# A gated mix of a long convolution and an MLP on one core: all 1,099 steps in a new order, with new evacuation engines and ring slots

## The chip, the core and the metric

The kernel runs on one core of a Trainium2 chip. A core has TensorE (PE) for matmuls, VectorE (DVE), ScalarE (ACT), GpSimd (POOL) and the queue of SyncE (SP), which here issues nearly all DMA transfers. Each engine works through its own list of instructions in order; semaphores make an instruction wait for what it reads or overwrites. The metric is the device time of one execution in microseconds (us). Lower is better. Names such as L707 are lines of the kernel's file.

## The reference, cut to what matters

```python
def _A_ref(q, k, v, shift_k, ssm_k, ssm_D):          # B, S, D = 1, 2048, 640
    for t in range(4):                                # causal 4-tap shift convolution of k
        k_shift = k_shift + k_pad[:, t:t + S, :] * shift_k[:, 3 - t][None, None, :]
    kv = k_shift * v
    ...
    y = irfft(rfft(kv, 2 * S) * rfft(ssm_k, 2 * S))[:S]   # long causal convolution, per channel
    y = y + kv * ssm_D[None, None, :]
    return q * y

def _B_ref(x, w1, w2, w3, w4):                        # w1, w2: 640x640; w3: 640x1536; w4: 1536x640
    h = _gelu(_layernorm(x) @ w1)
    hs = (the four quarters of h, shifted by 1, -1, 2, -2 in time) @ w2
    x1 = x + hs
    return x1 + _gelu(_layernorm(x1) @ w3) @ w4

x = A_q
g = _sigmoid((x * gate_w).sum(-1, keepdims=True))
return g * _A_ref(x, A_k, A_v, A_shift_k, A_ssm_k, A_ssm_D) + (1 - g) * _B_ref(x, B_w1, B_w2, B_w3, B_w4)
```

All tensors are bf16; the output is 1 x 2048 x 640. (B_x isn't used.)

## The kernel before

**Tiling.** Time (2048) is 128 partitions times 16 rows t1 (`NT`). The 16 rows come in four blocks c of four rows, a block being one 640 KB transfer. Channels are 5 groups of 128. A program of named steps does the work; a name such as `x_norm.2.AAVV:1` is the builder `x_norm`, its arguments (block 2, engines AAVV) and the number k of the step within it.

**Start-up, both branches.** `load_x0`, `load_x`, `k_load.c:0` and `v_load` bring in x, k and v. `x_stats` makes the layernorm's sums of a block, row by row: on DVE for a letter V, on ACT for a letter A as a square and a copy, each with a sum (L666 to L698); its last step raises to a power on POOL. `x_norm` writes the normalised rows, on ACT or DVE by letter. `x_turn` transposes a block into `xt`: for blocks 0 and 1 with PE and evacuations of up to eight 128 x 128 pieces (`transposed`, L610), for blocks 2 and 3 with the letter D as one DMA transposition on SP (L652). `k_load.c:1` to `:6` transpose a block of k in the same way, and `tap` forms the four-tap convolution of 128 channels with 76 small row-tiled matmuls (L590); each quarter of its result is multiplied by v either by DVE from PSUM (letter V, `both`, L605) or by an ACT copy (`copied`, L599) and a DVE product (`times`, L602). `mlp1.c.u` is one product of block c with 128 columns of w1 in PSUM, five matmuls (L707), and a gelu on ACT (L710).

**The long convolution** is a Fourier transform in two stages of matmuls. `step1.KV` and `step1.HT0` (filter: `load_h`, `h_transpose`) apply table F1 and send the results to scratch in DRAM, `S_x` and `S_h` (L437). `gather.x.s` and `gather.h.s` read them back transposed, 640 KB each, into a ring of four buffers "ax" (L440 to L446). `step2` applies table CMP, `product` multiplies the spectra, `step3` goes back by table INV and sends to `S_g`, `gin` reads that, `step4` applies F4 and multiplies by the gate and by q (`load_q`). The tables are made on the chip: `f1_table`, `t2_table`, `i_tables`, `f4_table` end in a sine on ACT (L277). Sine and gelu need different tables of ACT's own, which it loads when the function changes (ACT_TABLE_LOAD).

**The MLP.** `h_shift` on POOL shifts the quarters of h; `w2.t1` makes x1 in two halves, adds x on DVE (L791) and takes the squares' sum on ACT (L797). `x1_norm` ends with a DMA transposition into `x1t` (L821). `w3.c.f` is a product like mlp1, with gelu into `gt` (L840, L844); `w4.t1` sums 12 matmuls for each half row (L867) and adds to X1 on DVE (L870). `scale_x1`, `gate` and `store` finish.

**Order.** Python runs the steps in the order of the tuple `ORDER` (from L911, `emit` at L2022), inside `tc.manual_schedule` (L2034), so each engine's queue has its instructions in that order and nothing reorders them. A step that issues on several engines issues on all of them at its place. SP's transfers, stores and transpositions are one queue too.

**Ring slots.** `slot()` takes the next character of `SLOTS[tag]` each time a buffer with that tag is asked for: "c" are the eight PSUM banks, "row" four row buffers (k blocks, normalised rows, staging, gates), "gt" four gelu buffers, "xt" two, "gq" three, "ax" four gather buffers, "hp" four spectra. A buffer can be written once all readers of the tile that had this slot before are done; that wait is put on the instruction that writes first.

**Evacuation.** The letters A and V in a step's name choose ACT or DVE for each copy out of PSUM (`evac`, L358).

Of the kernel before, what the change touches and what calls it, by code (L numbers as in the profile page):

```python
# [41 lines left out]
def kernel(  # L42
# [836 lines left out]
    def step4(t1, ev):  # L879
# [32 lines left out]
        "open.L1.left:0 "  # L912
        "open.A2.right:0 "
        "consts0:0 "
        "load_x0.0:0 "
        "warm:0 "
        "load_x0.1:0 "
        "consts0:1 "
        "warm:1 "
        "warm:2 "  # L920
        "pow0:0 "
        "kv_alloc:0 "
        "k_load.3.AVA:0 "
        "f4_table:0 "
        "x_stats.0.VVVA:0 "
        "warm:3 "
        "k_load.3.AVA:1 "
        "x_stats.0.VVVA:1 "
        "load_x.1:0 "
        "x_stats.0.VVVA:2 "  # L930
        "k_load.3.AVA:5 "
        "x_stats.0.VVVA:3 "
        "x_stats.0.VVVA:4 "
        "x_stats.0.VVVA:5 "
        "x_stats.0.VVVA:6 "
        "warm:4 "
        "row_order:0 "
        "k_load.2.VAV:0 "
        "f1_table:0 "
        "x_norm.0.VVAA:0 "  # L940
        "x_norm.0.VVAA:1 "
        "f4_table:1 "
        "x_stats.1.VVVV:0 "
        "k_load.3.AVA:2 "
        "load_x.3:0 "
        "x_norm.0.VVAA:2 "
        "x_stats.1.VVVV:1 "
        "k_load.3.AVA:3 "
        "x_turn.0.AAA:0 "
        "k_load.3.AVA:6 "  # L950
        "k_load.2.VAV:5 "
# [1113 lines left out]
```

## Time and profile before

| | us |
|---|---|
| median of 3 runs | 227.58 (227.55 to 228.22) |
| the profiled execution | 227.13 |
| its span, first to last instruction | 225.4 |
| PE busy in the span | 217.8 |
| DVE busy | 183.7 |
| ACT busy | 171.4 |
| POOL busy | 38.1 |
| moved by DMA | 57.61 MB |

The granted TensorE clock is 1.000 over the span. In the views, "busy" is the time in which an engine executes; a group's row gives the line, engine, operation, output and input with shapes, the count, then busy time and mean of one in ns, then the idle time of the engine just before these instructions and what ended most of it. A row of the timeline gives start, duration, engine and line. In square brackets stand the idle time before an instruction and what released it. PEld is the loading of weights into PE, which overlaps its matmuls; SPq and ACTq are the queues' own times.

### The profile page before, as it was taken

The numbers are of one execution on the slowest core, as the hardware profiler recorded it, in microseconds if no ns is written. First come the engines' busy times: TensorE is split into PE (matmuls) and PEld (weight loads), VectorE is DVE, ScalarE is ACT, GpSimd is POOL, SyncE is SP. The second block draws the span as 40 slices with busy tenths as digits, with TensorE's granted clock in tenths as the row PEclk, the third lists the DMA queues.
The fourth block names the chain that finished last, engine by engine and source line by source line (L and its number), as shares of the span: only waits on it lengthen the run. The fifth ranks groups of instructions, "written<-read, shape, count | busy, mean of one in ns | idle before, by whom it ended". The sixth has DMA issues, their size and how long they took to land.

```text
span 225.4 us, 6053 instructions
## 1 busy us (share of the span) xinstructions
PE 217.8 (97%) x2427; PEld 121.5 (54%) x2428; DVE 183.7 (81%) x447; ACT 171.4 (76%) x341; POOL 38.1 (17%) x91
## 2 busy tenths in 40 slices
PE   8989999899999999999999999999999999999994
PEld 2557455447846563345664444556533547657762
DVE  7898998868889969963899988989999841439994
ACT  4899988787999999999987597967988450266450
POOL 4247246816000431300600000000000000000000
PEclk9999999999999999999999999999999999999999
DMA  6999998892998999999989570690794879429914
GB/s 226 374 376 344 258 280 170 317 364 107 361 365 355 348 295 265 410 334 343 254 219 338 116 243 0 191 379 17 119 305 166 249 259 366 175 60 305 324 70 179
DMA packets 41770, 57.61 MB, mean 256 GB/s; under 512 B 18446, under 2 KB 34446, under 8 KB 41486
## 3 DMA queue, kind: packets, MB, share of 16 engines
q1 hardware_dynamic: 41166, 54.60, 75.4%
q0 software_dynamic: 576, 2.62, 3.1%
q8 instruction: 19, 0.31, 0.6%
q14 instruction: 9, 0.07, 0.1%
HBM read 34.93 MB, written 18.35 MB: 236 GB/s over the span
## 4 chain that ended last, share of the span: by engine, by line
PE 79%; DMA 9%; DVE 4%; ACT 4%; issue 1%; POOL 1%; SPq 0%; ACTq 0%
PE ps L840 24%; PE ps L867 23%; PE psw L788 7%; PE ps L465 5%; PE ps L893 4%; DMA X<-in_A_q_dram 4%; PE psm L707 4%; DMA xt<-xn 3%; PE psz L228 3%; PE ps L512 3%; PE ps L423 2%; PE pst L390 2%; DVE X L791 2%; ACT stg L360 2%; DMA S_x<-stg 2%; PE psk L590 1%
## 5 line engine op out<-in xcount | busy, mean ns | idle before, releaser
L840 PE MATMUL ps<-x1t,W 128*128 128x512 bf16 x240 | 56.1, 380 | 0.1
L867 PE MATMUL ps<-W,gt 128*128 128x320 bf16 (+2 forms) x383 | 55.1, 299 | 0.1
L867 PEld LDWEIGHTS <-gt 128*128 128x128 bf16 x384 | 36.2, 98 | 17.7 <-issue 3.0
L844 ACT ACTIVATE gt<-ps 128x512 bf16<-128x512 f32 x48 | 27.6, 609 | 19.0 <-PE ps L867 10.6
L840 PEld LDWEIGHTS <-W 128*128 128x128 bf16 x240 | 21.9, 98 | 28.7 <-issue 5.9
L360 ACT CAST stg<-ps 128x512 bf16<-128x512 f32 x55 | 28.6, 604 | 2.3 <-PE ps L423 2.0
L870 DVE SCALAR_TENSOR_TENSOR X<-ps,OMG,X 128x320 bf16<-128x320 f32 (+2 forms) x32 | 17.2, 547 | 11.9 <-PE ps L867 11.7
L707 PE MATMUL psm<-xt,WA 128*128 128x512 bf16 x100 | 23.4, 379 | 1.9 <-DMA WA<-in_B_w_dram 0.8
L360 ACT CAST gs<-ps 128x320 bf16<-128x320 f32 x41 | 15.6, 440 | 8.8 <-PE ps L512 4.8
L788 PE MATMUL psw<-WA,HT 128*128 128x320 bf16 x116 | 21.4, 300 | 0.0
L362 DVE CAST XS<-ps 128x512 bf16<-128x512 f32 x19 | 12.5, 684 | 6.7 <-PE ps L465 6.7
L362 DVE CAST stg<-ps 128x512 bf16<-128x512 f32 x25 | 15.8, 683 | 1.9 <-PE ps L423 1.9
L707 PEld LDWEIGHTS <-WA 128*128 128x128 bf16 x100 | 9.2, 97 | 12.9 <-DMA WA<-in_B_w_dram 1.0
L360 ACT CAST hs<-ps 128x512 bf16<-128x512 f32 x28 | 15.0, 605 | 1.4 <-PE ps L465 1.4
L791 DVE SCALAR_TENSOR_TENSOR X<-psw,X 128x320 bf16<-128x320 f32 x32 | 14.5, 487 | 1.6 <-PE psw L788 1.6
L897 ACT ACTIVATE y<-ps,GS 128x320 bf16<-128x320 f32 x22 | 10.4, 526 | 5.7 <-PE ps L893 3.5
L710 ACT ACTIVATE HT<-psm 128x512 bf16<-128x512 f32 x20 | 11.8, 617 | 3.6 <-PE psm L707 3.5
L788 PEld LDWEIGHTS <-HT 128*128 128x128 bf16 x116 | 10.7, 98 | 6.8 <-issue 3.1
L362 DVE CAST gs<-ps 128x320 bf16<-128x320 f32 x23 | 10.7, 484 | 2.4 <-PE ps L512 1.7
L797 ACT ACTIVATE jk<-X 128x640 bf16<-128x640 bf16 x16 | 12.2, 761 | 0.5 <-DVE X L791 0.4
L788 PE MATMUL psw<-WA,HM 128*128 128x320 bf16 x44 | 12.3, 299 | 0.0
L360 ACT CAST XS<-ps 128x512 bf16<-128x512 f32 x21 | 11.8, 607 | 0.5 <-PE ps L465 0.3
(151 smaller groups left out, 346.6 us busy)
## 6 DMA issues: line engine op xcount, KB each, us to landing
S_x<-stg SPq DMA_DIRECT2D x8, 640.0 KB, 4.3
S_h<-stg SPq DMA_DIRECT2D x8, 640.0 KB, 4.8
ax<-S_x SPq DMA_DIRECT2D x8, 640.0 KB, 5.9
ax<-S_h SPq DMA_DIRECT2D x8, 640.0 KB, 8.1
S_g<-gs SPq DMA_DIRECT2D x8, 640.0 KB, 3.6
W<-in_B_w_dram SPq DMA_DIRECT2D x2, 1920.0 KB, 9.1
kn<-in_A_k_dram SPq DMA_DIRECT2D x4, 640.0 KB, 6.9
E<-in_A_ssm_k_dram SPq DMA_DIRECT2D x5, 512.0 KB, 6.1
```

The source lines that it names most:

```text
L360: A.copy(out=dst, in_=src)
L362: V.tensor_copy(out=dst, in_=src)
L465: PE.matmul(ps[j][q:q + 32, lo - 512 * u:hi - 512 * u], lhsT=CMP[HALF[j], 8 * b + 4 * h + i, c, :], rhs=st[name, 2 * b + h][HALF[j], i, lo ...
L707: PE.matmul(ps[:].rearrange("p (a b) -> p a b", a=4), lhsT=W1N[:, k, 160 * u:160 * u + P] if u < 4 else W1M[:, k, :], rhs=xt[:, :, k, :], ...
L710: A.activation(out=st["HT"][:, 4 * c:4 * c + 4, u, :], in_=ps[:].rearrange("p (t b) -> p t b", t=4), func=ACT.Gelu_apprx_tanh)
L788: PE.matmul(ps[:], lhsT=h_tile(f, t1), rhs=W2P[:, f, o:o + W], start=(f == 0), stop=(f == 4))
L791: V.scalar_tensor_tensor(out=X1[:, t1, o:o + W], in0=box["ps"][:], scalar=1.0, in1=X[:, t1, o:o + W], op0=ALU.mult, op1=ALU.add, accum_out ...
L797: A.activation(out=jk[:], in_=X1[:, t1, :], func=ACT.Square, accum_out=S12[:, 1, t1:t1 + 1])
L840: PE.matmul(ps[:].rearrange("p (a b) -> p a b", a=4), lhsT=st["W3"][:, k, f * P:(f + 1) * P], rhs=xt[:, :, k, :], start=(k == 0), stop=(k ...
L844: A.activation(out=st["gt", c, f // 4][:, f % 4, :], in_=ps[:], func=ACT.Gelu_apprx_tanh)
L867: PE.matmul(ps[:], lhsT=st["gt", c, f // 4][:, f % 4, i * P:(i + 1) * P], rhs=st["W4"][:, f, o:o + w], start=(f == 0), stop=(f == FC - 1))
L870: V.scalar_tensor_tensor(out=X1[:, t1, o:o + w], in0=box["ps"][:], scalar=OMG[:, t1:t1 + 1], in1=X1[:, t1, o:o + w], op0=ALU.mult, op1=ALU ...
```

## The change

Two places of the file change: `SLOTS` and `ORDER`. Every step of before is in the new order once, and none is added, but for the letters: how many evacuations of a kind ACT does goes, before to after, from 12 to 5 in `tap`, 22 to 17 in `step4`, 41 to 38 in `step3`, 21 to 19 in `step2.x`, 28 to 29 in `step2.h`, 27 to 25 in `step1.KV`, 28 to 29 in `step1.HT0`, 3 to 6 in `x_norm`, 6 to 8 in `x1_norm`, 3 to 5 in `x_turn`, 6 to 5 in `k_load` and 2 to 3 in `h_transpose`. The ring "gq" is asked for 22 times instead of 34, since each letter A of `tap` and `step4` needs a buffer. The slots are dealt anew: each new buffer takes the one that has been free longest at its place in the order. The number of buffers stays.

```diff
     SLOTS = {
-        "c": "012345670124703510347205142356401723605162370514731057423671045261304732641374153670421350627413"
...
+        "c": "012345670254602167053253210657432170413547021630627501432675140326573410267451306427103542673542"
...
-        "row": "01230213021302320123012031203120310310303",
-        "gt": "012301031010231012301201",
+        "gt": "012302201231230102312301",
+        "row": "01230213201320312031023122103120321021020",
         "xt": "010101",
-        "gq": "0120201201021020120122102121021021",
-        "ax": "0123120312030213",
-        "hp": "01231302",
+        "gq": "0122010200120201021012",
+        "ax": "0123031203123120",
+        "hp": "01230312",
     }
```

Of the order, the new one in its core (the old one is printed one step to a line from L911):

```diff
+        "open.L1.left:0 open.A2.right:0 kv_alloc:0 warm:0 load_x0.1:0 warm:1 consts0:0 consts0:1 warm:2 warm:3 "
+        "warm:4 load_x0.0:0 f4_table:0 load_x.3:0 k_load.0.AAA:0 k_load.0.AAA:3 x_stats.0.VVVA:0 x_stats.0.VVVA:1 "
+        "x_stats.0.VVVA:2 x_stats.0.VVVA:3 load_x.1:0 f4_table:1 x_stats.0.VVVA:4 k_load.0.AAA:1 x_stats.0.VVVA:5 "
+        "k_load.0.AAA:5 x_stats.0.VVVA:6 k_load.3.VVV:0 x_stats.3.VVAA:0 x_stats.3.VVAA:1 x_stats.3.VVAA:2 "
+        "x_stats.3.VVAA:3 x_stats.3.VVAA:4 x_stats.3.VVAA:5 x_norm.0.AVAV:0 x_norm.0.AVAV:1 x_turn.0.AAA:0 "
+        "x_norm.0.AVAV:2 x_norm.0.AVAV:3 x_turn.0.AAA:4 k_load.0.AAA:2 k_load.1.AVA:0 row_order:0 x_turn.0.AAA:5 "
+        "x_stats.1.VVVV:0 x_stats.1.VVVV:1 x_stats.3.VVAA:6 k_load.3.VVV:3 k_load.3.VVV:1 x_stats.3.VVAA:7 "
+        "x_turn.0.AAA:2 x_turn.0.AAA:1 k_load.3.VVV:4 k_load.1.AVA:5 x_turn.0.AAA:3 x_stats.1.VVVV:2 k_load.1.AVA:6 "
...
+        "k_load.0.AAA:4 k_load.1.AVA:4 k_load.3.VVV:2 load_w1.0:0 mlp1.0.0:0 mlp1.0.0:1 k_load.3.VVV:6 "
+        "x_norm.1.VVAV:0 mlp1.0.1:0 v_load.0:0 x_norm.1.VVAV:1 x_norm.1.VVAV:2 x_norm.1.VVAV:3 k_load.0.AAA:6 "
+        "load_w1.1:0 mlp1.0.3:0 w1_mixed:0 k_load.2.VVV:0 k_load.2.VVV:5 k_load.2.VVV:3 k_load.2.VVV:1 "
+        "x_turn.1.VAA:4 z_cols:0 x_turn.1.VAA:2 mlp1.0.1:1 x_turn.1.VAA:5 x_turn.1.VAA:3 x_norm.3.VVVA:0 mlp1.0.3:1 "
+        "x_norm.3.VVVA:1 x_turn.1.VAA:0 x_norm.3.VVVA:2 x_norm.3.VVVA:3 mlp1.0.4:0 x_turn.1.VAA:1 v_load.1:0 "
+        "mlp1.0.4:1 mlp1.1.0:0 k_load.1.AVA:2 k_wrap:0 mlp1.1.2:0 mlp1.1.0:1 mlp1.1.1:0 load_cj:0 mlp1.1.2:1 "
+        "k_load.2.VVV:2 mlp1.1.1:1 k_load.2.VVV:6 k_load.2.VVV:4 kv_consts:0 tap.3.AVVA:0 tap.3.AVVA:7 tap.4.AVVV:0 "
+        "tap.3.AVVA:1 tap.4.AVVV:5 tap.4.AVVV:3 tap.4.AVVV:1 load_x.2:0 x_turn.3.D:0 mlp1.1.4:0 x_stats.2.VVAA:0 "
+        "tap.3.AVVA:3 mlp1.3.0:0 x_stats.2.VVAA:1 x_stats.2.VVAA:2 x_stats.2.VVAA:3 x_stats.2.VVAA:4 v_load.2:0 "
...
+        "x_stats.2.VVAA:7 load_w2:0 load_h.2:0 load_h.1:0 tap.3.AVVA:4 mlp1.3.0:1 d_fold:0 mlp1.3.3:0 mlp1.3.3:1 "
+        "mlp1.3.4:0 mlp1.3.4:1 h_shift.3:0 tap.3.AVVA:2 tap.0.AVVV:0 x_norm.2.AAVV:0 x_norm.2.AAVV:1 "
+        "x_norm.2.AAVV:2 h_shift.0:0 tap.0.AVVV:5 tap.0.AVVV:7 tap.0.AVVV:8 tap.1.VVAV:0 tap.1.VVAV:1 tap.1.VVAV:3 "
+        "tap.1.VVAV:7 mlp1.0.2:0 tap.1.VVAV:5 tap.0.AVVV:1 x_norm.2.AAVV:3 mlp1.3.1:0 tap.1.VVAV:2 tap.0.AVVV:6 "
+        "mlp1.0.2:1 f1_table:1 tap.1.VVAV:4 h_shift.3:1 tap.2.VVVV:0 tap.2.VVVV:1 tap.2.VVVV:7 tap.0.AVVV:3 "
+        "tap.0.AVVV:4 mlp1.3.1:1 mlp1.1.3:0 mlp1.1.3:1 tap.0.AVVV:2 tap.1.VVAV:8 tap.1.VVAV:6 "
+        "step1.KV.3.AAVAAAVVAV:6 step1.KV.3.AAVAAAVVAV:7 tap.2.VVVV:3 x_turn.2.D:0 tap.2.VVVV:2 mlp1.2.3:0 "
+        "step1.KV.3.AAVAAAVVAV:8 mlp1.2.3:1 mlp1.2.0:0 tap.2.VVVV:4 load_h.4:0 mlp1.2.0:1 tap.2.VVVV:5 tap.2.VVVV:6 "
...
+        "gather.x.0:0 step2.x.0.AVVVAAVVAV:13 w2.14:0 w2.9:1 w2.14:1 i_tables:6 w2.11:0 w2.11:1 w2.13:2 "
+        "step2.x.3.AVVVVVAAVV:7 w2.4:2 swap.L1.L2.left:0 w2.4:3 w3.0.11:0 w3.0.1:0 w2.8:4 w3.0.4:0 w3.0.3:0 w2.6:4 "
+        "w3.0.11:1 w3.0.1:1 w2.13:3 gate:0 w3.0.4:1 step2.x.3.AVVVVVAAVV:1 step2.x.3.AVVVVVAAVV:12 "
...
+        "step2.x.3.AVVVVVAAVV:14 w2.10:4 w2.11:4 w2.9:4 x1_norm.2.VAAA:0 x1_norm.2.VAAA:1 step2.x.0.AVVVAAVVAV:7 "
+        "step2.x.0.AVVVAAVVAV:1 step2.x.0.AVVVAAVVAV:11 step2.x.0.AVVVAAVVAV:10 step2.x.0.AVVVAAVVAV:3 "
+        "step2.x.0.AVVVAAVVAV:5 w3.0.10:0 w3.0.7:0 w3.0.10:1 w3.0.7:1 w3.0.9:1 w3.0.6:0 load_w4:0 x1_norm.2.VAAA:2 "
+        "w3.0.5:0 w3.0.6:1 step2.x.3.AVVVVVAAVV:3 scale_x1.3.V:0 step2.x.3.AVVVVVAAVV:4 gather.h.7:0 "
+        "step2.h.3.AVAAVAAVAV:12 step2.h.3.AVAAVAAVAV:14 step2.x.3.AVVVVVAAVV:5 step2.x.3.AVVVVVAAVV:9 w3.0.5:1 "
+        "w4.2:0 step2.x.3.AVVVVVAAVV:10 step2.h.3.AVAAVAAVAV:13 step2.x.0.AVVVAAVVAV:4 x1_norm.1.VVAV:2 "
+        "x1_norm.1.VVAV:3 step2.x.3.AVVVVVAAVV:11 gather.h.6:0 step2.h.3.AVAAVAAVAV:3 step2.h.3.AVAAVAAVAV:9 "
...
+        "step2.h.3.AVAAVAAVAV:1 w4.1:1 gather.h.0:0 step2.h.3.AVAAVAAVAV:2 step2.h.0.AAAAAAAAAA:0 "
+        "step2.h.0.AAAAAAAAAA:1 step2.h.0.AAAAAAAAAA:2 product.7:1 product.7:2 scale_x1.8.V:0 product.7:3 "
+        "gather.h.1:0 product.7:4 step2.h.0.AAAAAAAAAA:12 w4.0:2 w4.0:3 step2.h.0.AAAAAAAAAA:14 "
...
+        "step2.h.2.AVAVAVAVAA:6 step2.h.2.AVAVAVAVAA:7 step2.h.2.AVAVAVAVAA:8 w4.5:2 w4.5:3 step2.h.2.AVAVAVAVAA:11 "
+        "w4.6:0 w4.6:1 x1_norm.3.VAAA:6 w4.7:0 step3.2.VVVVAAAA:5 step3.2.VVVVAAAA:8 step2.h.2.AVAVAVAVAA:10 "
+        "w3.2.5:0 w3.2.8:0 w3.2.6:0 product.5:0 w3.2.5:1 step3.2.VVVVAAAA:7 step3.2.VVVVAAAA:6 pow0:0 "
...
+        "w4.13:3 step4.12.AA:6 store.6:0 w4.15:0 w4.15:1 w4.15:3 store.7:0 w4.14:0 w4.14:1 w4.14:2 w4.14:3 "
+        "store.8:0 store.8:1 close.L2:0 close.C:0"
```

SP's first transfers, before: `load_x0.0`, `load_x0.1`, `k_load.3`, `load_x.1`, `k_load.2`, `load_x.3`, `load_w1.1`, `load_w1.0`, `k_load.0`, `k_load.1`, `load_x.2`, `load_cj`, `d_fold`, `x_turn.3.D`. After: `load_x0.1`, `load_x0.0`, `load_x.3`, `k_load.0`, `load_x.1`, `k_load.3`, `k_load.1`, `load_w1.0`, `load_w1.1`, `k_load.2`, `load_cj`, `load_x.2`, `x_turn.3.D`, `load_gw`, `load_w2`, `load_h.2`, `load_h.1`, `d_fold`, `x_turn.2.D`. PE's nine products of mlp1 ahead of `tap.3` become seven, and `pow0`, which stood among the first steps, is now one of the later ones.

More of the change, by code (lines that the diff above doesn't have):

```diff
@@ L911 @@
     ORDER = (
[L912 to L951, printed above, removed]
@@ L2008 @@
-        "store.8:1 "
-        "close.L2:0 "
-        "close.C:0 "
[170 rows of a table added]
     ).split()
```

1064 lines of the change are left out of this document (4 added, 1060 removed), and 127 rows, old and new, of the table ORDER.

## The prediction, made before the changed kernel ran

> **What bounds the kernel now.** I read the page's busy shares first, then the stretches of the span, then what TensorE (PE) waits for, then the chain that ended last and the first 42 us line by line.
>
> ```profile
> PE 217.8 (97%) x2427; PEld 121.5 (54%) x2428; DVE 183.7 (81%) x447; ACT 171.4 (76%) x341; POOL 38.1 (17%) x91
> PE 79%; DMA 9%; DVE 4%; ACT 4%; issue 1%; POOL 1%; SPq 0%; ACTq 0%
> ```
>
> PE is busy 97% of the span, and 79% of the last chain is PE. The change keeps every matmul, so what it can win is PE's idle time and little else. The stretches (start:end, length, busy time of PE, PEld, DVE, ACT, POOL, granted clock, DMA share, GB/s) say where that is.
>
> ```profile
> 0.98:8.30 7.32, 7.32 (x21) 2.59 (x21) 6.59 (x35) 4.57 (x8) 2.92 (x9) 1.00 0.85 304
> 8.30:14.20 5.90, 4.39 (x64) 3.69 (x63) 5.28 (x19) 5.24 (x7) 0.51 (x4) 1.00 1.06 378
> 14.20:27.70 13.50, 13.48 (x105) 7.77 (x105) 12.66 (x38) 13.44 (x27) 7.43 (x10) 1.00 1.02 325
> 27.70:41.50 13.80, 12.39 (x412) 7.80 (x412) 12.83 (x37) 12.10 (x25) 8.71 (x23) 1.00 0.92 223
> 41.50:85.00 43.50, 43.40 (x357) 25.96 (x358) 35.86 (x104) 38.79 (x76) 11.73 (x21) 1.00 0.89 318
> 85.00:130.00 45.00, 44.85 (x515) 21.93 (x512) 37.33 (x76) 39.22 (x81) 6.52 (x21) 1.00 0.94 282
> 130.00:221.40 91.40, 91.34 (x964) 51.32 (x955) 72.00 (x141) 57.79 (x123) 0.00 (x0) 1.00 0.62 202
> ```
>
> Idle is 1.51 us in 8.3 to 14.2 (5.90 less 4.39), 1.41 in 27.7 to 41.5, and 0.10, 0.15 and 0.06 in the three long stretches, 0.31 together. So about 3.2 us could be won. In the first two stretches the DMA engines are full (share 1.06 and 0.92), and ACT is busy 13.44 of 13.50 us between them: the start-up hangs on transfers and on ACT, the other 180 us on PE alone.
>
> ```profile
> PE psm L707 <- DMA WA<-in_B_w_dram: 0.8, 1, 0.8
> PE psm L707 <- ACT yk L599: 0.8, 1, 0.8
> PE pst L619 <- DMA kn<-in_A_k_dram: 0.7, 1, 0.7
> PE psm L707 <- DMA xt<-xn: 0.2, 1, 0.2
> ```
>
> Transfers cost PE 0.8, 0.7 and 0.2, thus 1.7 us: all that a plan with longer transfers can save here.
>
> **The start-up, step by step.** Before, x0, k.3, x.1, k.2, x.3 and the w1 halves are loaded in that order; after, x0, x.3, k.0, x.1, k.3, k.1, w1. The arrivals are read off the first instruction that waited for each:
>
> ```profile
> 4.36 0.74 ACT L679 ACTIVATE jk<-X 128x640 bf16<-128x640 bf16 x1 [2.36 <-DMA X<-in_A_q_dram]
> 5.22 0.74 ACT L681 ACTIVATE jk<-X 128x640 bf16<-128x640 bf16 x1
> 8.29 0.86 PE L619 MATMUL pst<-IDB,kn 128*128 128x128 bf16 x12
> 9.85 0.89 DVE L685 BATCH_NORM_STATS2 b<-X 128x6 f32<-128x320 bf16 x2 [0.32 <-DMA X<-in_A_q_dram]
> 11.42 0.68 PEld L619 LDWEIGHTS <-kn 128*128 128x128 bf16 x12 [0.89 <-DMA kn<-in_A_k_dram]
> 14.22 3.41 PE L707 MATMUL psm<-xt,WA 128*128 128x512 bf16 x15 [0.82 <-DMA WA<-in_B_w_dram]
> ```
>
> The third transfer is there at 8.3, the fourth at 9.85, the fifth at 11.4. In the changed kernel the third is x.3, and its four statistics passes on ACT (x_stats.3, two blocks of a square and a sum) stand ahead of x_norm.0. A pass takes 0.86 from start to start (4.36 to 5.22), so ACT is free at 8.3 + 4 × 0.86 = 11.7. Behind them wait, on ACT, two of x_norm.0's rows and the copies that free x.0's transposes for mlp1:
>
> ```profile
> 9.97 0.82 ACT xn L662
> 10.79 0.47 ACT KT L360
> 12.09 0.91 ACT xt L360
> 24.32 7.63 DMA xt<-xn
> 32.00 3.41 PE psm L707 x15
> 41.46 2.33 PE psm L707 x10
> ```
>
> Two rows 1.64, two half copies and three whole ones, 2 × 0.47 + 3 × 0.91 = 3.2: 16.6 for the first product against 14.22 before. By then PE has done one more block of K transposes:
>
> ```profile
> 20.26 1.32 PE L619 MATMUL pst<-IDB,kn 128*128 128x128 bf16 x20
> ```
>
> that is 1.32 us of the 2.4. Seven products at 1.1 and two blocks of 20 transposes at 1.2 to 1.3 bring tap.3 to 16.6 + 7.7 + 2.4 = 26.7 (before 27.7, with nine products done).
>
> Then x.3's transposition. It is issued behind x_norm.3's last row, on SP behind load_cj and load_x.2. On ACT and DVE the queue sums put that row's end at 24.25, as early as before (24.32). But before, ten products and two taps were over when PE needed it (32.00); after, eight products and two taps are, and PE arrives at about 30.0. I give this transposition the 7.63 us of the chain's row, since it is issued at the same time into the same traffic: it lands at 31.9, and PE waits 1.9. The bounds come from the six transpositions there are, by the tile views: first the two of x (issued at 24.3 and 34.7), then the four of x1 (78 to 159).
>
> ```profile
> DMA to landing us min/median/max: 6.6/7.1/7.6
> DMA to landing us min/median/max: 4.9/5.1/6.3
> ```
>
> x.2's comes next, as before (34.7). Its rows 0 and 1 (x_norm.2, now on ACT) stand behind the gelus of four products that only start at 31.9: 31.9 + 4 × 1.1 + gelu 0.6 + two rows 1.64 = 38.55 for the issue. PE, meanwhile, has 11.3 us of work ready and comes to mlp1.2.3 at 43.2. By 4.9 us the transposition lands at 43.4, by 7.6 at 46.2; I take 6.1, near the middle of both rows, 44.65. To set that against before: summing PE's units at their trace prices, before stood at 36.5 us of work at 41.46 (4.96 behind), and after stands at 37.1 at 44.65 (7.55 behind). The start-up costs 7.55 - 4.96 = **+2.6**. With both transpositions at 4.9 PE waits for neither in full: the first lands at 29.15, ahead of PE, the second is issued at 36.65 and lands at 41.55, and the term is 41.55 - 37.1 - 4.96 = -0.5. With the second at 7.6 it is +4.1.
>
> Hidden work in this stretch: the second sine of f1_table now stands between gelus and brings two more table loads.
>
> ```profile
> 18.62 1.28 ACT L710 ACT_TABLE_LOAD   x1
> 19.92 2.06 ACT L710 ACTIVATE HT<-psm 128x512 bf16<-128x512 f32 x4
> ```
>
> 2 × 1.28 = 2.6 us of ACT at about 40 to 44, while PE has taps and then waits for x.2's transposition; without that cover up to 2.6 would come on top. The Trainium skill ("ScalarE: Activation LUTs", section "What ACT_TABLE_LOAD costs") has about 1283 ns for the load and some 1380 ns of draining, 2.66 us a switch. The load agrees with the row; the draining does not show, as the gelu follows 0.02 us after the load's end. By the page the two would take 5.3 us, and by an estimate from it 2.7 us more would come in front of mlp1.2.0's bank, of which the wait hides most.
>
> **The middle.** Three places have less cover than before.
>
> First, ACT at the start of w3. The squares of the last w2 rows and the last sine table now stand right ahead of the first gelus.
>
> ```profile
> L797 ACT ACTIVATE jk<-X 128x640 bf16<-128x640 bf16 x16 | 12.2, 761 | 0.5 <-DVE X L791 0.4
> L844 ACT ACTIVATE gt<-ps 128x512 bf16<-128x512 f32 x48 | 27.6, 609 | 19.0 <-PE ps L867 10.6 <-PE ps L840 8.2
> L277 ACT ACTIVATE INV<-n,NPI 128x512 bf16<-128x512 int32 x3 | 2.2, 730 | 0.0
> ```
>
> Sine 0.73, two squares 1.52, table load 1.28, three gelus 1.83, one copy 0.5: 5.9 us, while PE has 3.8 to 4.9 us before it needs their banks. Behind are the gelus for w3.0.8 and on. 0 if ACT comes early, 2.5 if it is also late by the table load's 1.28 and a copy; I take 5.9 - 4.9 = **1.0**.
>
> Second, gather.h.7. Its ring slot (ax 0) was x.1's and comes free with step2.x.0:3; PE then has four w3 products (4.4) and 0.2 until step2.h.3:12 reads it. On SP it stands right behind load_w4. The tile view of ax has for all 16 gathers:
>
> ```profile
> DMA to landing us min/median/max: 5.3/6.0/8.2
> ```
>
> Landing after 6.0 costs 6.0 - 4.6 = **1.4**; the ends are 0.7 and 3.6. Third, gather.h.1 (slot of x.7, free after step2.x.3:9) has 6.3 us of PE until step2.h.0:12: 0 by the median, 1.9 by 8.2. I take 0. The middle is **+2.4**, with 0 and 8.0 (all at their ends) as bounds.
>
> **What is won.** Fewer changes between row-tiled and whole-array groups of matmuls (46 for 48), and units summed by their trace prices give 213.6 us of PE for 214.2: **-0.4** (0 to -1). The 0.3 of idle after 41.5 may go: **-0.3**. Twelve evacuations lose their copy on ACT:
>
> ```profile
> L599 ACT CAST yk<-psk 128x512 bf16<-128x512 f32 x12 | 6.5, 604 | 0.5 <-PE psk L590 0.5
> L602 DVE TENSOR_TENSOR KV<-yk,KV 128x512 bf16<-128x512 bf16 x12 | 5.9, 520 | 0.8 <-ACT yk L599 0.8
> L605 DVE TENSOR_TENSOR KV<-psk,KV 128x512 bf16<-128x512 f32 x8 | 5.3, 679 | 0.0
> ```
>
> A tap's quarter by ACT and DVE costs 604 and 520 ns, by DVE alone 679. That takes 0.8 of wait from the list above (already in the start-up's sum), and ACT loses some 3 us, DVE gains about 2; neither is the bound over the long stretches. The three filter loads behind x.2's transposition, h_shift on POOL, load_w4 and pow0 have 3 us or more of PE between their end and their reader and are put at nothing; where that cover is gone they show as waits of step 1 on HT0 or of w2.
>
> **Sum.** 227.13 (the profiled execution; its span is 225.4) + 2.6 + 2.4 - 0.4 - 0.3 = 231.4. The profiled run is 0.45 under the median of 227.58, so for the median 231.9.
>
> **The rivals.**
> *The middle's waits do not come* (ACT early, gathers covered because PE itself comes later): 231.9 - 2.4 = 229.5. For it: the same gathers cause no PE wait today. Against: today h.7 has more than four products in front.
> *Short transfers, not slower than before.* If both transpositions land in under about 5.5 us, PE waits for neither, -0.5; with gathers at 5.3 the middle is 0.7; 227.13 - 0.5 + 0.7 - 0.7 = 226.6, and 227.1 for the median. For it: the later four had 4.9 to 6.3, median 5.1. Against: the two in the start-up, at a DMA share of 0.92, had 6.6 and 7.6.
> *Both gathers at 8.2*: 3.6 + 1.9 in place of 2.4, 235.0. For it: load_w4's 1.9 MB is just ahead of h.7. Against: the median.
> *PE turns cold once more.* The first matmuls go at 0.43 from start to start, the later ones at half of it:
>
> ```profile
> 1.38 0.15 PEld L228 LDWEIGHTS <-WZ 128*128 128x128 bf16 x1 [0.28 <-issue]
> 1.81 0.15 PEld L228 LDWEIGHTS <-WZ 128*128 128x128 bf16 x1 [0.28 <-issue]
> 6.87 0.96 PEld L228 LDWEIGHTS <-WZ 128*128 128x128 bf16 x5 [0.21 <-issue]
> ```
>
> If a longer wait in the start-up brought that back for the 5.5 us that it lasts here (1.38 to 6.87), half of it, 2.8, is lost: 234.7. The longest gap of today, 0.8 to 0.9, didn't. The Trainium skill ("TensorE: Matmul & The Clock Gate", Part 1) has half rate after an idle window of about 3.4 us; by that a wait of 1.9 would be safe, and the clock of 1.00 in all stretches agrees.
> *It does what it says*: the 1.7 us of transfer waits go and none come: 227.6 - 1.7 - 0.4 = 225.5.
>
> **How the numbers follow.** Forecast 0.42, no middle waits 0.20, short transfers 0.14, slow gathers 0.14, cold PE 0.05, as it says 0.05. Differences under 0.3% (0.7 us) are no change here. Faster: 0.05 + 0.06 of the short transfers + 0.01 = 0.12; same 0.06; slower 0.82. The range 227.1 to 236.0 takes in all but the last case and a good third of those at its ends; the forecast's own is 229.5 to 234.
>
> **What would show it.** Right: a first product at 16 to 17 us with ACT's x_stats sums ahead; a PE wait of 1 to 2 us for xt near 30 and another near 43; no PE wait on WA or yk; a wait of step2.h.3 for ax near 105. Wrong: transpositions landing in 5 us, a first product at 14, or a granted clock under 1.00 after 30 us. It falls if PE's idle up to mlp1.2.3 isn't larger than today's.

## The result, and the profile after

The changed kernel takes 237.5 us in the median of four runs (236.24 to 240.97), the kernel before 227.9 on the same chip (227.55 to 228.29). The ratio is 1.0402, 95% interval 1.0353 to 1.0451: slower by 9.6 us, against a forecast of 4.3 and outside its range. Ratios, here and below, leave out executions that fell into a slower state (240.97 is one), while medians take in all; the profiles of fill, prod_first, old_h1 and loads_late are of such slower executions. The profiled execution took 237.36, its span is 235.5, 10.1 more than before's 225.4.

The page of the changed kernel, busy shares and the chain's shares by engine:

```profile
PE 219.4 (93%) x2427; PEld 123.5 (52%) x2428; DVE 187.8 (80%) x445; ACT 173.0 (73%) x333; POOL 39.4 (17%) x91
PE 69%; DMA 16%; ACT 6%; DVE 5%; issue 2%; SPq 1%; ACTq 0%; DVEq 0%
```

PE does the same 2,427 matmuls in 219.4 instead of 217.8 us, so 1.6 of the 10.1 us is slower work and 8.5 is idle time. Where the idle time lies shows if both spans are cut at the same times (not at the same work: the changed kernel is behind at each cut). A row is start:end, length, busy time of PE, PEld, DVE, ACT, POOL, granted clock, DMA share, GB/s. First the kernel before, in windows of its own:

```profile
0.00:45.70 45.70, 41.78 (x621) 23.35 (x623) 40.80 (x134) 38.49 (x70) 23.72 (x56) 1.00 0.94 295
45.70:130.00 84.30, 84.06 (x849) 46.39 (x848) 69.87 (x172) 75.12 (x151) 14.42 (x36) 1.00 0.91 296
130.00:194.00 64.00, 63.99 (x782) 33.67 (x772) 50.34 (x81) 43.14 (x93) 0.00 (x0) 1.00 0.67 216
194.00:226.00 32.00, 27.94 (x191) 18.06 (x189) 22.65 (x61) 14.65 (x30) 0.00 (x0) 0.99 0.49 166
```

Then the changed kernel:

```profile
0.00:45.70 45.70, 38.48 (x600) 23.92 (x600) 36.55 (x119) 37.46 (x62) 17.44 (x46) 0.93 0.88 263
45.70:130.00 84.30, 82.05 (x821) 45.06 (x819) 72.43 (x179) 77.13 (x150) 18.02 (x39) 1.00 0.89 299
130.00:194.00 64.00, 64.00 (x793) 32.42 (x778) 53.16 (x87) 45.16 (x97) 3.93 (x6) 1.00 0.63 190
194.00:236.00 42.00, 34.86 (x234) 22.12 (x232) 25.67 (x63) 13.25 (x26) 0.00 (x0) 1.00 0.53 196
```

Length less PE's busy time, before and after: 3.92 and 7.22 us up to 45.7; 0.24 and 2.25 from there to 130; 0.01 and 0.00 to 194; in the last stretch, taken to the span's end (225.4 and 235.5), 3.46 and 6.64. The gain in idle time is **3.3 + 2.0 + 0 + 3.2 = 8.5**. The 1.6 of slower work is a balance, counted along PE's time: 2.6 more for the 120 transposes of the start-up, part of which ran at a granted clock of 0.5 (the first stretch has 0.93), 1.4 less for the first 23 matmuls, since they went at full rate from about 4.05 us on and not from 6.79, and 0.4 more elsewhere. So waits were added in three places, and for the third, at the end, the prediction had no term.

What PE waited for in the changed kernel (engine, line, releaser: total, times, longest):

```profile
PE ps L893 <- DMA gin<-S_g: 1.9, 1, 1.9
PE psm L707 <- DMA xt<-xn: 1.8, 1, 1.8
PE pst L619 <- DMA kn<-in_A_k_dram: 1.6, 1, 1.6
PE psk L590 <- issue: 1.4, 1, 1.4
PE pst L619 <- ACT xn L662: 1.4, 1, 1.4
PE ps L893 <- DVE X L870: 1.3, 1, 1.3
...
PE ps L840 <- DMA x1t<-xn: 1.0, 1, 1.0
PE ps L423 <- DVE stg L362: 1.0, 2, 0.7
```

The waits for kn, xn, xt and "issue" are the start-up's, those of L840 (w3) and L423 (step1) the middle's, and the two of L893 (step4) the end's. Of the last four groups none was in before's list. The start-up on PE, line by line:

```profile
9.19 1.33 PE L619 MATMUL pst<-IDB,kn 128*128 128x128 bf16 x20 [1.57 <-DMA kn<-in_A_k_dram]
11.92 1.46 PE L619 MATMUL pst<-IDB,xn 128*128 128x128 bf16 x12 [1.40 <-ACT xn L662]
15.73 2.46 PE L619 MATMUL pst<-IDB,kn 128*128 128x128 bf16 x24
18.04 3.40 PE L707 MATMUL psm<-xt,WA 128*128 128x512 bf16 x15
32.95 4.49 PE L707 MATMUL psm<-xt,WA 128*128 128x512 bf16 x20 [1.82 <-DMA xt<-xn]
38.63 0.45 PE L590 MATMUL psk<-DG,KT 32*128 32x128 bf16 x20
40.51 0.49 PE L590 MATMUL psk<-DG,KT 32*128 32x128 bf16 x28 [1.44 <-issue]
```

The first block of k is the fourth transfer and not the third, and the first row of x waits for ACT: 1.57 and 1.40 us. From 10.88 to 17.70 us PE runs at half its clock: 12 transposes take 1.46 us and 24 take 2.46, where 20 took 1.32 before. The first product comes at 18.04. The transposition of x.3 holds PE for 1.82 at 32.95. The stop at 40.51 is in the middle of a quarter of a tap; no semaphore releases it.

The end. SP's queue (start, length, line, operation), and PE around the last products of w3 (L840), then step4 (L893):

```profile
206.76 4.26 PE L840 MATMUL ps<-x1t,W 128*128 128x512 bf16 x19
210.87 1.52 PE L893 MATMUL ps<-gin,F 128*128 128x320 bf16 x10
...
211.06 2.45 SPq L537 DMA_DIRECT2D gin<-S_g  x4
...
220.56 1.79 PE L893 MATMUL ps<-gin,F 128*128 128x320 bf16 x12 [1.93 <-DMA gin<-S_g]
```

`gin.1` is a tile in the memory of w3's weights (L532: tag "W3"), so it can be fetched only when the last w3 product is over, at 211.0; its four transfers are issued from 211.06 on. Its first reader is step4.10. In the new order PE has 7.6 us of work between the last w3 product (211.03) and that reader (it came at 218.64 and waited). In the old order the first reader is step4.11, with 10.1 us in front, from 200.25 to 210.31. The chain of before has it (start, length, engine, line, count):

```profile
200.25 5.16 PE ps L893 x38
205.42 4.89 PE ps L867 x36
210.31 1.90 PE ps L893 x14
```

The tile view of gin, after and then before, shows what a transfer needs:

```profile
DMA to landing us min/median/max: 4.0/5.3/7.5
```

```profile
DMA to landing us min/median/max: 2.6/4.1/5.7
```

The longest, 7.5, is the last transfer in the chain (212.91, the issue of the last quarter, to 220.43). The other wait of L893, 1.29 us up to 197.34, had two causes that ended together. gin.0.2, whose first reader stands right behind it in the new order, landed at 197.09. The PSUM bank of that reader came free with an addition of w4 on DVE, which ended at 197.10, and the list names this one ("DVE X"). An earlier landing alone would not have ended the wait.

### The profile page after: what moved, and what is told of

Its sections match the earlier page's. It is cut to its first block, busy times and chain, and to the rows that moved or that the text cites. A ratio compares the mean times of both kernels' runs of the same rounds, so it can differ in the third digit from the quotient of the medians.

```text
span 235.5 us, 6036 instructions
## 1 busy us (share of the span) xinstructions
PE 219.4 (93%) x2427; PEld 123.5 (52%) x2428; DVE 187.8 (80%) x445; ACT 173.0 (73%) x333; POOL 39.4 (17%) x91
## 4 chain that ended last, share of the span: by engine, by line
PE 69%; DMA 16%; ACT 6%; DVE 5%; issue 2%; SPq 1%; ACTq 0%; DVEq 0%
PE ps L840 23%; PE ps L867 19%; PE psm L707 6%; DMA x1t<-xn 5%; PE pst L619 4%; PE ps L465 4%; PE psw L788 3%; DMA gin<-S_g 3%; DMA xt<-xn 3%; PE ps L893 3%; PE ps L512 3%; DMA X<-in_A_q_dram 3%; ACT stg L360 2%; PE pst L390 2%; PE ps L423 2%
## 5 line engine op out<-in xcount | busy, mean ns | idle before, releaser
L840 PE MATMUL ps<-x1t,W 128*128 128x512 bf16 x240 | 55.9, 380 | 1.1 <-DMA x1t<-xn 1.0
L840 PEld LDWEIGHTS <-W 128*128 128x128 bf16 x240 | 21.9, 98 | 29.0 <-issue 5.2
L897 ACT ACTIVATE y<-ps,GS 128x320 bf16<-128x320 f32 x17 | 8.1, 526 | 19.9 <-PE ps L893 19.5
L360 ACT CAST gs<-ps 128x320 bf16<-128x320 f32 x38 | 14.8, 443 | 7.4 <-PE ps L512 6.1
L362 DVE CAST XS<-ps 128x512 bf16<-128x512 f32 x21 | 13.8, 683 | 6.6 <-PE ps L465 6.6
L362 DVE CAST stg<-ps 128x512 bf16<-128x512 f32 x26 | 16.9, 682 | 2.5 <-PE ps L423 1.4
L360 ACT CAST hs<-ps 128x512 bf16<-128x512 f32 x29 | 15.7, 598 | 2.9 <-PE ps L465 2.9
L362 DVE CAST gs<-ps 128x320 bf16<-128x320 f32 x26 | 11.5, 484 | 3.4 <-PE ps L512 2.0
L893 PE MATMUL ps<-gin,F 128*128 128x320 bf16 x64 | 10.2, 299 | 3.2 <-DMA gin<-S_g 1.9
```

The source lines that it names most:

```text
L360: A.copy(out=dst, in_=src)
L362: V.tensor_copy(out=dst, in_=src)
L840: PE.matmul(ps[:].rearrange("p (a b) -> p a b", a=4), lhsT=st["W3"][:, k, f * P:(f + 1) * P], rhs=xt[:, :, k, :], start=(k == 0), stop=(k ...
L893: PE.matmul(ps[:], lhsT=F4[:, r].rearrange("p a b -> p (a b)"), rhs=g[:, r, o + 320 * v:o + 320 * v + 320], start=(r == 0), stop=(r == 1))
```

## The experiments

The theory: three separate losses that add up, in the start-up, in the middle and at the end, the last by gin's two readers. The rivals: one cause upstream (the half clock, or the start-up's wait for x.3) that shifts everything behind it, and the choice of PSUM banks. To take them apart, parts of the two orders are joined. A hybrid keeps, on either side of a cut, the relative order and letters of one kernel; the rings other than "c" are dealt by the rule of the longest free buffer.

**The PSUM banks first: banks_dealt, h_start, h_rest, h_end.** The first hybrids needed a bank list of their own, so I also ran the changed kernel with its list made by the same rule as theirs, "c" dealt by the order of the last readers:

```diff
-        "c": "012345670254602167053253210657432170413547021630627501432675140326573410267451306427103542673542"
+        "c": "012345670254602167053253125431026715072301645726734165075203754216302547103654270631742561263045"
```

> The changed kernel with one thing different: the eight PSUM banks are dealt by the rule that its other rings follow (the bank whose last reader stands earliest in the order), instead of by the plan's own list. It is the control for the next three, which need a list of banks of their own. If the plan's choice of banks is worth nothing: 237.5, within 1 us. If banks matter: over 239.

> The steps that the changed kernel has ahead of 56.7 us (the third product pair of the first transform of block 1) stand in the old relative order, with the old evacuation engines; everything behind is as in the changed kernel. PE's delay against the sum of its units is 8.9 us there in the changed kernel and 5.0 in the old one. Theory (each stage's delay stays its own): 3.9 us are won, 233.6. Rival (a later start is taken up by later waits for transfers, which then grow): 236.5 or more.

> The counterpart: the changed kernel up to 56.7 us, and all later steps in the old relative order with the old evacuation engines. Theory: the later part brought 6.4 us of delay, less what the old one has there (2 us), so 231 to 232. Rival: 234.5 or more, since the old later order was planned for an earlier start.

> The changed kernel up to 194 us (w4.11:2), and all later steps in the old relative order. Theory: the waits of 1.45 us for gin.0.2 and 2.09 us for gin.1 come from too little PE work between the last step3 or the last w3 and the first step4 that reads them; with ten more us of PE work there they go, 237.5 - 3.5 = 234.0. Rival: these transfers are slow (7.5 us against 4) whatever stands in front, and PE waits elsewhere: 236.5 or more.

Measured: banks_dealt 248.06 us, ratio to before 1.0895 (1.079 to 1.1); h_start (old start, new rest) 248.34, 1.0906; h_rest (new start, old rest) 245.32, 1.0801; h_end (old end) 245.44, 1.0736. The list alone costs 10.6 us over the changed kernel, as much as the change under study; against banks_dealt only h_end stands out, at the edge of its interval. The waits of banks_dealt show how a bank does it:

```profile
PE ps L465 <- DVE X L870: 2.8, 1, 2.8
```

step2 (L465) waits 2.8 us for a bank whose reader is an addition of w4 on DVE, another stage altogether. (So the rule that each new buffer takes the one free longest at its place in the order describes the other rings of the changed kernel, whose lists came out the same here; the banks of "c" follow a list of their own.) The hybrids were repeated with each bank from the list of the kernel that its part comes from.

**The end undone: h_end2.** From w4.11:2 on (194 us) the old order with its letters and banks, ahead of it the changed kernel:

```diff
-        "gin.0.2:0 step4.4.VA:0 step4.4.VA:1 w3.3.3:1 gin.2.1:0 step4.6.VA:0 step4.6.VA:3 step4.6.VA:1 step4.1.VA:3 "
...
+        "w3.3.10:1 gin.0.2:0 step4.6.AV:3 step4.3.AV:3 w3.3.9:1 step4.3.AV:4 w3.3.7:1 step4.4.AV:3 step4.1.VA:0 "
```

> As h_end (changed kernel up to 194 us, then the old relative order), with the banks of the kernel that each part comes from. Theory: the two waits for gin (1.45 and 2.09 us) go, 234.0. Rival: PE waits for them elsewhere, 236.5 or more.

Measured: 233.66, ratio 1.0199 (1.01 to 1.0297). The old end gives 2.0% back, about 4.6 us; the two intervals together leave some 2 to 7. Its tile view of gin, and its longest waits of PE:

```profile
DMA to landing us min/median/max: 4.7/5.7/7.4
```

```profile
PE psm L707 <- DMA xt<-xn: 1.8, 1, 1.8
PE pst L619 <- ACT xn L662: 1.5, 1, 1.5
PE ps L423 <- DVE stg L362: 1.4, 3, 0.7
PE psk L590 <- issue: 1.4, 1, 1.4
```

The transfers of gin are no quicker (median 5.7, after 5.3; longest 7.4, after 7.5) and still PE waits neither for them nor for the bank: what lost time is what stands in front of the readers, not the transfer. Order, letters and banks of the end were put back together, so their shares are not told apart. The start-up's waits remain, as they should.

**The half clock: fill.** Thirteen more matmuls on zeros keep PE busy where it waited before 17.7 us:

```diff
-        for n in (11, 3, 3, 3, 3):
+        for n in (11, 3, 3, 3, 3, 7, 6):
...
-        "x_stats.3.VVAA:3 x_stats.3.VVAA:4 x_stats.3.VVAA:5 x_norm.0.AVAV:0 x_norm.0.AVAV:1 x_turn.0.AAA:0 "
+        "x_stats.3.VVAA:3 x_stats.3.VVAA:4 x_stats.3.VVAA:5 x_norm.0.AVAV:0 x_norm.0.AVAV:1 warm:6 x_turn.0.AAA:0 "
```

> The changed kernel with 7 more matmuls of the warming kind in PE's wait for k's first block (7.5 to 9.2 us) and 6 in its wait for x_norm.0 (10.5 to 11.9); they write the warming bank and nothing reads them. In the changed kernel's profile the granted clock was 0.5 from 10.9 to 17.7 us and the transposes there took 2.4 us more than at full rate. Theory A: these waits brought the half rate and it costs its 2.4 us: no stretch below 1.00, 235.1. Rival B: the wait for x.3's transposition (2.0 us near 31) sets the end of this stage, so the clock stays at 1.00 but that wait grows to 4: 236.5 or more. Rival C: the clock falls all the same.

Measured: 238.86, ratio 1.0394 (1.0296 to 1.0493), the changed kernel's time within the interval, whose low end just reaches Theory A's 235.1. A window of fill, one of the changed kernel over the same stretch, and PE's line at the transposition of x.3 in fill:

```profile
11.00:18.00 7.00, 6.73 (x76) 4.79 (x74) 6.76 (x25) 6.98 (x9) 3.56 (x5) 1.00 1.00 293
```

```profile
11.00:18.00 7.00, 6.08 (x60) 6.08 (x61) 5.53 (x21) 5.99 (x9) 3.07 (x4) 0.52 0.83 249
```

```profile
32.89 4.49 PE L707 MATMUL psm<-xt,WA 128*128 128x512 bf16 x20 [2.68 <-DMA xt<-xn]
```

In this window the clock stays at 1.00 and PE does 76 matmuls in the place of 60, but the first product of x.3 starts at 32.89, in the changed kernel at 32.95: the time won is spent in a longer wait for the same transposition. The profile of fill has a half clock elsewhere, from 42.29 to 45.70, behind a stop of 2.1 us, so half rate was moved and not removed there. But the one execution of fill with a mean clock of 1.000 took 238.87, and the three with 0.993 took 237.25, 238.85 and 240.91. The half clock in the start-up was real, and taking it away won nothing.

**Products into the wait: prod_first.** If PE waits 1.8 us for x.3, two products that are ready could go in front (mlp1.0.2 and mlp1.1.3, moved from behind tap.0 and tap.1):

```diff
-        "mlp1.0.4:1 mlp1.1.0:0 k_load.1.AVA:2 k_wrap:0 mlp1.1.2:0 mlp1.1.0:1 mlp1.1.1:0 load_cj:0 mlp1.1.2:1 "
+        "k_wrap:0 mlp1.1.2:0 mlp1.1.0:1 mlp1.1.1:0 mlp1.0.2:0 mlp1.1.3:0 load_cj:0 mlp1.1.2:1 k_load.2.VVV:2 mlp1.1.1:1 "
```

> The changed kernel with two products of x.0 and x.1 (mlp1.0.2 and mlp1.1.3) and their gelus moved from behind x.3's products to in front of the first taps, so that nine products stand there as in the old order; x.3's transposition then finds PE busy. Theory A (the start is a chain through ACT and the two transpositions): PE's wait of 2.0 us for x.3 goes, but the same time is waited before x.2's first product, and the ratio stays at 1.037 to 1.043. Rival B (the wait is a matter of PE's order alone): 2 us less, 1.031.

Measured: 238.24, ratio 1.0333 (1.0234 to 1.0433). The wait for x.3 is gone from the list, and others are there: the stop between taps grows to 1.8, and a wait for a gelu on ACT of 1.1 is new. In the profile the time comes back behind it; the ratio's interval holds both Theory A and Rival B, so how much was won stays open.

**The start alone and the middle alone.** Cuts at 57 us (h_start2, h_rest2) and then at the first product of x.2, 45.7 us: h_start3 has the old start-up, h_rest3 the new one with everything else old, h_mid3 the new middle alone.

> As h_start (old relative order and old evacuation engines up to 56.7 us, the rest as in the changed kernel), but each PSUM bank as the kernel has it that the part comes from, so that the list of banks is no longer part of the difference. Theory (each stage keeps its own delay): 3.9 us less than the changed kernel, 233.6. Rival (later waits take the start up): 236.5 or more.

> As h_rest (changed kernel up to 56.7 us, then the old relative order), with the banks of the kernel that each part comes from. Theory: 231 to 232. Rival: 234.5 or more.

> The cut of h_start2 lay where the old order has other fillers between the transforms. Here it lies at the first product of x.2 (45.7 us in the changed kernel, 41.5 in the old one), where PE has done the same units in both: what comes ahead stands in the old order with the old engines and banks, all behind as in the changed kernel. PE's delay there was 8.7 us in the changed kernel and 5.0 in the old one. Theory (each stage keeps its delay): 3.7 us less than the changed kernel, a ratio to before of 1.040 - 0.016 = 1.024. Rival (later transfers wait for other things and PE meets them): 1.035 or more.

> The counterpart with the same cut: the changed kernel up to the first product of x.2, all behind in the old order with the old engines and banks. Theory: the later part's 9.05 us of delay go back to the old 2.0, less 0.6 of PE units that the new order saves: 6.4 us less, a ratio of 1.012. Rival (the old later order was planned for transfers and evacuations of its own start): 1.03 or more, as with the other cut.

> The old order up to the first product of x.2 and again from 194 us on (the cut of h_end2); only the middle, 46 to 194 us, as in the changed kernel. Theory: the middle's own waits, 3.1 us, stay: 1.040 - 0.016 (start) - 0.016 to 0.020 (end) = 1.004 to 1.008. Rival: parts that were not planned together cost more than each saves, 1.02 or more.

Measured: h_start2 237.74, 1.0379; h_rest2 237.56, 1.0333; h_start3 238.54, 1.0367; h_rest3 232.19, **1.0124 (1.005 to 1.0197)**; h_mid3 235.73, 1.0275. Only h_rest3 met its expectation: the new start-up alone costs 1.24%, 2.8 us, by the interval 1.1 to 4.5. (Its profile also has a wait of 1.2 us for w4's weights at 111 us, which neither kernel has, so part of this may be the joint's.) The four others have waits that neither kernel has. At 57 us PE waits 2.0 us in h_rest2 for the shift of h on POOL. In h_start2 it waits 1.2 and 0.8 us at 54 and 56 us for staging rows, but also 1.4 us at 22 us for an evacuation on DVE and 1.0 at 34.7 with no releaser, both inside the old start-up and at no joint. In h_start3 and h_mid3 the cut put a filter load (load_h.1, 512 KB) ahead of x.2's transposition, and PE stopped in a tap:

```profile
38.52 0.95 PE L590 MATMUL psk<-DG,KT 32*128 32x128 bf16 x33 [2.46 <-issue]
```

**That load alone: old_h1, old_h1b, loads_late.** The kernel before, with one line moved, and the changed kernel with its three loads behind the transposition of x.2:

```diff
+        "load_h.1:0 "
         "load_gw:0 "
...
-        "load_h.1:0 "
```

```diff
-        "x_stats.2.VVAA:7 load_w2:0 load_h.2:0 load_h.1:0 tap.3.AVVA:4 mlp1.3.0:1 d_fold:0 mlp1.3.3:0 mlp1.3.3:1 "
+        "x_stats.2.VVAA:7 tap.3.AVVA:4 mlp1.3.0:1 d_fold:0 mlp1.3.3:0 mlp1.3.3:1 "
```

> The kernel before with one transfer issued earlier and nothing else: the filter's second 512 KB (load_h.1) goes from behind x.2's transposition to behind load_h.2, some 8 us earlier; nobody waits for it sooner. In every run with w2 and two filter loads ahead of that transposition PE stopped for 1.4 to 2.5 us within the second of the two adjacent taps, always at the same place of its instruction stream, with no semaphore to wait for, some 1.5 us after a late 16 KB packet of an instruction queue. Theory: the loads delay the fetch of PE's instructions; here the stop appears too (the kernel before has none there) and costs 1.5 to 2.5 us: ratio 1.006 to 1.012. Rival: the stop belongs to the new order, and the transfer's place does nothing: within 0.3% of before.

> The changed kernel with the three transfers (load_w2, load_h.2, load_h.1) issued behind x.2's transposition instead of ahead of it. Theory of the fetch: the stop of 1.4 us in tap.1 goes. What it is worth: PE then reaches x.2's first product about when its transposition lands (45.6 in the changed kernel), so that half or more comes back as a wait there: ratio 1.033 to 1.040. If the stop stays, the loads are not its cause.

> A second look at old_h1 (one filter load issued 8 us earlier in the kernel before), whose profiled execution was one of its longest. Theory: the fetch of a 16 KB block of instructions again starts later than it does in the kernel before (34.0 us), and PE stops without a semaphore at the same place of its stream (before its instruction 705 or 961, which are one block of 256 apart).

Measured: old_h1 231.51, ratio 1.0109 (1.0035 to 1.0183). In the profile of old_h1b, the same kernel looked at once more (229.09, before 228.11), and in that of before, the same quarter of tap.0:

```profile
36.59 0.39 PE L590 MATMUL psk<-DG,KT 32*128 32x128 bf16 x15
37.69 0.58 PE L590 MATMUL psk<-DG,KT 32*128 32x128 bf16 x33 [0.71 <-issue]
```

```profile
36.60 0.82 PE L590 MATMUL psk<-DG,KT 32*128 32x128 bf16 x48
```

PE is at the same place at the same time in both and nothing it reads was changed; with the load in front it stops. The edit costs 1%, but how much of that is the stop is not told apart: the profile of old_h1b also waits 2.7 us for k, where before waits 0.7, well ahead of the moved load, and old_h1's has a stop of 3.5. loads_late takes 245.44, 1.0649 (1.0541 to 1.0758): the stop is gone, but PE then waits 3.7 us for the filter's load (E, L390), which the new order needs early. (Its profile also has two waits of 2.6 and 2.5 us ahead of the moved loads that the changed kernel hasn't, so not all of the 8 us is theirs.) It was forecast at 1.033 to 1.040, a miss: the stop could not be removed for nothing by moving the loads.

**The joints mended: h_start4, h_mid4, h_mid5.** h_start4 and h_mid4 leave load_h.1 behind x.2's transposition; h_mid5 (old start, new middle, old end) also puts the step1.KV.3:6 to :8 that stood right behind tap.1 behind the first two products of x.2, as PE would else wait for their input:

```diff
-        "step1.KV.3.AAVAAAVVAV:6 step1.KV.3.AAVAAAVVAV:7 tap.2.VVVV:3 x_turn.2.D:0 tap.2.VVVV:2 mlp1.2.3:0 "
...
+        "mlp1.2.3:0 mlp1.2.3:1 mlp1.2.0:0 step1.KV.3.AAVAAAVVAV:6 step1.KV.3.AAVAAAVVAV:7 step1.KV.3.AAVAAAVVAV:8 "
```

> As h_start3, with x.2's transposition and load_h.1 in their old relative order too (in h_start3 the cut had put load_h.1 ahead, and PE stopped for 2.5 us in tap.0). Theory: without that stop the start takes its old time and the rest keeps the new delay: 1.024. Rival: 1.035 as in h_start3.

> As h_mid3, with the same correction: old start, new middle (46 to 194 us), old end. Theory: the middle's own 3.1 us of waits, less 0.6 of PE units: 1.008 to 1.012. Rival: above 1.02.

> h_mid4 with one joint mended: there the first transform (step1.KV.3:6) stood directly behind the last tap, whose products DVE had not done, and PE waited 2.7 us for DVE, which neither kernel does; here x.2's first two products stand in between. Old start, new middle, old end. Theory: 1.024 less 2.7 us is 1.012, which is the middle's own share. Rival: the middle hides a wait of its own behind that one, 1.02.

Measured: h_start4 235.86, 1.0254 (1.0145 to 1.0364), near its 1.024, and h_mid4 233.59, 1.0237 (1.015 to 1.0324), a miss; both have a joint's wait of 2.6 us (step1 for KV on DVE), so neither number is clean; h_mid5 231.27, **1.0116 (1.0034 to 1.0197)**. In the profile of h_mid5 the start is in before's order and the middle in the changed kernel's:

```profile
0.00:45.70 45.70, 41.81 (x621) 23.59 (x621) 39.46 (x128) 39.06 (x72) 18.08 (x46) 1.00 0.93 295
45.70:130.00 84.30, 82.04 (x835) 45.59 (x835) 73.01 (x179) 76.81 (x153) 19.12 (x41) 1.00 0.88 289
```

Idle 3.89 in the first stretch (before 3.92) and 2.26 in the second (after 2.25): the middle loses its 2 us whether or not the start-up is late, though not in the same shares (1.5 for staging rows and 0.6 for x1t, in the changed kernel 1.0 and 1.0).

**The sum.** Start 1.24% (h_rest3), middle 1.16% (h_mid5), end 2.03% (1.0402 less 1.0199, h_end2): 4.4% together, about 2.8 + 2.6 + 4.6 us, against 4.02% measured. The parts add up within their intervals, each of which is some 0.7 to 1.1% wide either way, so this is a loose agreement. None of the three intervals reaches 0, but the start-up's and the middle's come near it (0.5 and 0.3%); that each has its own wait rests on the profiles as well. No combination ran faster than the kernel before, and none is to be expected from these parts, as each is a loss.

## Why the prediction was right in its direction and wrong in its size

**The step that failed is the list of places with less cover.** "The middle: three places have less cover than before" and the term -0.3 for the idle after 41.5 left the end at nothing. There the new order puts two readers of gin nearer to their transfers: step4.4 right behind gin.0.2, with 3.1 us of PE between the issue (192.92) and its arrival (196.05) against a landing of 4.2, and step4.10 with 7.6 us of PE behind the memory's release where 10.1 stood in front of the first reader before. It is the arithmetic that the prediction made for gather.h.7 (cover against landing time), and it was not made for gin. For gin.1, rows of before would have given 1.9 us until the last quarter is issued and up to 5.7 to land, 7.6 against a cover of 7.6: no margin left, but no wait yet (the landings of gin.1's own last two quarters are not told in that trace). It became one because the last quarter took 7.5. Measured: waits of 1.93 and 1.29 in the profile, 3.2 together, and 4.6 (2 to 7) by h_end2.

**The account in the profile's terms.** The sum had 4.7 us of added waiting (2.6 + 2.4 - 0.3) and -0.4 of work; measured are 8.5 and +1.6. Of the 3.8 us of waiting that the sum lacked, 3.2 are the end, 0.7 the start-up, and 0.3 the idle that was to go and did not, while the middle had 0.4 less. The 2.0 us of work that it lacked are mostly the transposes at half clock (2.6), which it had only as a rival, less the earlier full rate at the start (1.4); but fill shows that without the half clock the same time is waited.

**Start-up, +2.6 forecast.** Alone it measures 2.8 (h_rest3, 1.1 to 4.5). The prediction's own measure gives more: at the first product of x.2, at 45.73 in the profile, PE has 37.1 us of units behind it and is 8.6 late, 3.7 more than the 4.96 of before. The interval holds both, so the size is right only within a wide bound. The mechanism holds for its first half: x.3's transposition was to land at 31.9 and hold PE for 1.9; it was issued at 25.66 and took 7.25, and held PE for 1.82 up to 32.95. The second half was wrong. x.2's transposition was to hold PE at about 43; it was issued at 39.98 (forecast 38.55), took 5.6, and was there 0.2 us before PE came at 45.73. What held PE instead was the stop in the taps, 1.44, which is no wait for any engine. The two more table loads on ACT came (42.84 and 44.55), and PE did not wait behind them.

The first product was forecast for 16.6. The sum of copies there is wrong: 2 x 0.47 + 3 x 0.91 is 3.7 and not 3.2, which makes it about 17.1; the total does not hang on it, since x.3's transposition comes later. It came at 18.04 with the half clock and at 15.71 in fill without it (15.6 to 15.8 in four other profiles without it), so ACT's part was over-estimated by about 1 us.

**"PE turns cold once more", given 0.05, happened**, in another place and by shorter gaps than that rival had. The clock fell at 10.88, after a wait of 1.57 us (7.62 to 9.19) and 0.36 us into the next one of 1.40; the windows have 0.52 for 11 to 18 us. The Trainium skill ("TensorE: Matmul & The Clock Gate", Part 1) gives half rate after an idle window of about 3.4 us, and by that I called a wait of 1.9 safe. The trace does not agree: in the 3.41 us ahead of 10.88, PE was idle for 1.93 and busy for the rest. The price of that rival, 2.8 us, is wrong as well, as fill shows: 2.4 us of slower transposes vanish in the next wait.

**The middle, +2.4 forecast, 2.6 measured (h_mid5), by other waits.** PE did not wait for ACT at the start of w3, nor for either gather. gather.h.7 landed 4.3 us after its issue; I had put 6.0, with 5.3 as the low end. The tile view of ax in the changed kernel:

```profile
DMA to landing us min/median/max: 4.3/6.1/8.6
```

The waits that came are in the list above: 1.0 of step1 for staging rows on DVE and 1.0 of w3 for the transposed x1t. Together they are the 2.0 of the windows. The size was right by chance.

**What was won.** No waiting of before was saved on balance: the waits for WA (a transfer) and yk (ACT) went, as forecast, and a longer one for kn (a transfer) and a new one for xn (ACT) came.

**The condition for falling** (PE's idle up to the first product of x.2 not larger than before's) was not met: 7.22 against 3.92.

## What to carry to other kernels

Compare orders with one table over the whole program: for each buffer that a transfer fills, the PE work between the moment when it comes free and its first reader, against the time until its last part is issued plus the longest landing of that tile in the trace, with a margin, as landings move with the order (gin: up to 5.7 before, 7.5 after); here the place left out was where the largest loss lay. In this case time won early (fill) was waited again at the next arrival, while undoing the waits near the end gave time back (h_end2). When parts of two orders are joined, look first at the joint's own waits and at the bank list, or their cost is read as that of the part.

## What the hardware did that I had not expected

**PE can stop with no semaphore, right behind a packet of an instruction queue.** In 12 of the 20 profiles PE stopped between 0.7 and 2.5 us inside adjacent taps, always ahead of its recorded instruction 961, and in two at a product ahead of 705, which is 256 earlier (old_h1 3.5 us, h_start2 1.0). Three shorter stops of 0.2 to 0.35 us stand ahead of 961 too (h_mid4, h_mid5, h_start4). The page has 19 packets on a queue of its own, for 0.31 MB, thus 16 KB each:

```profile
q8 instruction: 19, 0.31, 0.5%
```

By the trace's packet records PE resumed 2.5 to 2.9 us after such a packet had started in the first 14, and 3.2 to 3.4 after it in the three short ones: in the changed kernel 37.95 and 40.51, in fill 38.24 and 40.95, in h_start3 35.61 and 38.52. In the kernel before that packet came at 34.0, PE reached the place at 36.84, and nothing stopped. So the stop looks like a late fetch of instructions in a stretch where 152 instructions (76 matmuls and their weight loads) pass in 0.92 us; that the fetch is the mechanism is argued from these coincidences. The transfer ahead of it is a strong sign and no full cause: with load_h.1 ahead of x.2's transposition all 13 profiles have a stop of 0.7 us or more, with it behind one of 7 has (h_start2).

**The half clock came on a grid of 3.41 us.** In each profile the changes of the granted clock lie whole multiples of 3.41 us apart (in the changed kernel 4.05, 10.88 and 17.70). Each of the 20 traces can be cut on its own grid, here from about 8 us on and up to the last 13 us or so. All 18 windows at full clock in which PE was idle for 1.92 us or more in sum were followed by a half clock; of those with 1.80 to 1.91 us it was three of seven; of all with less, one (in h_start, after 0.72). So two waits that share a window can count as one long wait, and the same waits on another phase of the grid may cost nothing: h_rest2 waited 1.25 and 1.55 us at almost the same places and kept 1.00.

**The order in which PSUM banks are dealt can matter as much as the order of the steps**: 10.6 us between two lists for the same 1,099 steps (banks_dealt).
